# TensorE's unrolled program becomes a loop of seven turns over five heads, and the batch moves into partition halves

## The chip, the core and the metric

One core of a Trainium2 chip runs the kernel in one launch. The metric is device time in microseconds (us). Everything is fp32.

## The reference, cut to what matters

One decoding step for a batch of 2. The row x of 512 values is normalised. The attention has 32 heads of 128 values and looks at the last 2048 positions of a cache of 8192. A bilinear gated unit runs beside it, and both are added to x.

```python
q = (x @ wq).reshape(B, Sq, Hq, Dh)                  # B, Sq, D = 2, 1, 512; Hq, Dh = 32, 128
k, v = k_cache[:, :, Sk - W:, :], v_cache[:, :, Sk - W:, :]     # W = 2048
p = softmax(einsum("bhqd,bhkd->bhqk", q, k) * Dh ** -0.5)
o = einsum("bhqk,bhkd->bhqd", p, v)
attention = o.reshape(B, Sq, Hq * Dh) @ wo
glu = ((x @ w_gate) * (x @ w_up)) @ w_down           # F = 1376
xn = layernorm(x);  out = x + attention(xn) + glu(xn)
```

One head has 2 MB of keys and 2 MB of values for both batch elements together. 159.5 MB are read in all, and each value is used once.

## The kernel before, in words

**Data.** The host lays all inputs out as one stream in the order of use. `blocks()` (line 57) lists its blocks, `pump()` (line 297) loads them with one DMA each, issued by SP, into three slots of SBUF of 7.9 MB (`step`). The next load of a slot is issued when everything in it has been used (`done`, line 318). `KS` (line 40) says how many heads of keys each load has, one to three; values (`vp`) fill the rest, a few heads behind the keys. A small block `first` with x and a part of wq goes ahead of them.

**A head.** Each partition has 16 positions of each of the two batch elements. VectorE multiplies the keys by q, which TensorE has laid out over all partitions in PSUM (`products`, line 432), and adds up each position's 128 products (`sums`, line 440). `maxima` (line 445) takes the largest score of each partition and GpSimd the largest over all partitions; `weights` (line 453) has ScalarE form the exponentials p, and GpSimd their sum. `reciprocals` (line 468) follows one head later.

**Values.** TensorE multiplies p with the values, eight matmuls of 512 columns to a head (`weigh`, line 484), in four column groups of one bank. ScalarE copies the bank to SBUF (`copy_out`, line 494), TensorE adds the four groups up and turns them (`transpose`, line 501), ScalarE scales by the reciprocals (into `oT`), and TensorE multiplies by the head's rows of wo into `acc` (`project_o`, line 520). One or two heads share a pass (`groups`).

**q.** For four heads at a time, one head's share of wq at a time (`project_q`, line 415), straight into one of two PSUM banks from which VectorE reads.

**Order.** All engines' programs are written out. The order in which `products`, `sums`, `weigh` and so on are called is the order on each engine's queue; `Flow` (line 109) finds the data dependences and puts semaphore waits on the instructions. Ahead of the last heads the order is written by hand, from the line `h = H - 2` on, with `keep_busy` (line 481), matmuls whose results nobody reads. There, head 31's values are multiplied in two column halves into two banks, and the rest of w_down (`down`, line 605) follows.

Of the kernel before, what the change touches and what calls it, by code (L numbers as in the profile page):

```python
# [8 lines left out]
ALU = mybir.AluOpType  # L9
# [8 lines left out]
J = W // P  # L18
# [6 lines left out]
LAG = 3  # L25
# [5 lines left out]
HG = 4  # L31
GC = HG * DH
JG = J // 4
CK, CQ, CO = B * J * DH, NC * GC, D
CP = CQ // NC
UNIT = CK + max(CP, CO)
STEP = 31 * FB
NP = 6
NV = CK // FB
KS = [3, 1, 2, 1, 2, 2, 1, 2, 2, 2, 1, 2, 2, 2, 1, 2, 2, 1]  # L40
WD = [(0, 2), (2, 4), (4, 7), (7, NFC - 1), (NFC - 1, NFC)]
NS = 3
BUFS = 3
BASE = 30 * 1024
FX = FR // NS

# [10 lines left out]
def blocks():  # L57

    def wd(n):
        return [("wd", i, D) for i in range(*WD[n])]

    def k(h):
        return [("k", h, CK)] + ([("wq", h, CP)] if h + HG < H else [])  # L70

    def v(h):
        return [("v", h, CK), ("wo", h, CO)]

    def gu(half):
        n = NC * (FH[half][1] - FH[half][0])
        return [("wg", half, n), ("wu", half, n)]

    ones = [("pick", 0, 8 * B), ("rows", 0, NFB * B)]
    first = [("x", 0, B * NC)] + ones + [("w", 0, NC * DH)]  # L80
    ahead = [[("w", 1, CQ - NC * DH)], gu(0) + gu(1), [("wr", 0, NS * P)] + wd(0)]
    pieces = [(h, n) for h in range(H - 1 - LAG) for n in range(NV + 1)]
    loads, h = [], 0
    for i, n in enumerate(KS):
        fields = (ahead[i] if i < len(ahead) else []) + sum((k(h + j) for j in range(n)), [])
        h += n
        room = (STEP - sum(w for _, _, w in fields)) // FB if i > 1 else 0
        taken, pieces = pieces[:room], pieces[room:]
        for g in sorted({g for g, _ in taken}):
            assert g < h - n  # L90
            ns = [m for t, m in taken if t == g]
            parts = [m for m in ns if m < NV]
            if parts:
                p0, p1 = parts[0], parts[-1] + 1
                fields.append(("vp", (g, p0, p1), FB * (p1 - p0)))
            if ns[-1] == NV:
                fields.append(("wo", g, CO))
        assert not pieces or pieces[0][0] >= h - NP
        loads.append(fields)
    assert not pieces and h == H - 1  # L100
    loads += [k(H - 1) + v(H - 1 - LAG) + wd(1)]
    out = [(("f", 0), first)] + [(("s", i), fields) for i, fields in enumerate(loads)]
    late, last = ("s", len(loads)), ("s", len(loads) + 1)
    out += [(late, v(H - 3)), (late, v(H - 2)), (last, [("v", H - 1, CK)])]
    out += [(last, [("wo", H - 1, CO)] + wd(2))]
    return out + [(last, wd(n)) for n in range(3, len(WD))]


class Flow:
# [7 lines left out]
    def __init__(self, nc):  # L117
        self.nc = nc
        self.units = {
            "pe": nc.tensor, "dve": nc.vector, "act": nc.scalar, "pl": nc.gpsimd, "sp": nc.sync,  # L120
        }
        self.ops, self.seen, self.free = [], {}, {}
        self.low = -(-nc.sbuf_base // 32) * 32
# [38 lines left out]
    def add(self, unit, make, writes, reads):  # L162
        n = len(self.ops)
        deps = set()
        for aps, write in ((reads, False), (writes, True)):
            for ap in aps:
                if not isinstance(ap.tensor, (bass.SBTensorHandle, bass.PSumTensorHandle)):
                    continue
                name, p0, p1, f0, f1 = self.box(ap)
                kept = []  # L170
                for old in self.seen.get(name, []):
                    m, w, a0, a1, b0, b1 = old
                    if m != n and (write or w) and a0 < p1 and p0 < a1 and b0 < f1 and f0 < b1:
                        deps.add((m, w))
                        if write and p0 <= a0 and a1 <= p1 and f0 <= b0 and b1 <= f1:
                            continue
                    kept.append(old)
                self.seen[name] = kept + [(n, write, p0, p1, f0, f1)]
        self.ops.append((unit, make, deps))
# [3 lines left out]

    def emit(self):
        nc, ops = self.nc, self.ops
        place, count = [], {}
        for n, (unit, make, deps) in enumerate(ops):
            key = ("dma", n) if make[0] == "dma_start" else unit
            count[key] = count.get(key, 0) + 1
            place.append((key, count[key]))  # L190
        knows = [None] * len(ops)
        known = {unit: {} for unit in self.units}
        waits = []
        for n, (unit, make, deps) in enumerate(ops):
            have = known[unit]
            need = {}
            for m, wrote in deps:
                key, at = place[m]
                if key == unit and (unit == "pe" or unit in ("dve", "act") and not wrote):
                    continue  # L200
# [7 lines left out]
            ]  # L208
            for m in keep:
# [11 lines left out]
        told = {m for keep in waits for m in keep} | {len(ops) - 1}  # L221
        sems, value, at = {}, {}, {}
        order = sorted({place[m][0] for m in told}, key=lambda key: (key in ("dve", place[-1][0]), str(key)))
        if order[-1] != place[-1][0]:
            order.append(order.pop(-2))
        for key in order:
            sems[key] = nc.alloc_semaphore("done_" + (key if isinstance(key, str) else f"load{key[1]}"))
# [7 lines left out]
        for n, (unit, (method, args, kwargs), _) in enumerate(ops):  # L235
            eng = self.units[unit]
            keep = sorted(
                waits[n], key=lambda m: (isinstance(place[m][0], tuple) and m >= landed, m)
            )
            landed = max([landed] + [m for m in keep if isinstance(place[m][0], tuple)])  # L240
# [5 lines left out]
            if n in value:  # L246
                key = place[n][0]
                made.then_inc(sems[key], 16 if isinstance(key, tuple) else 1)
            if n == len(ops) - 2:
# [5 lines left out]
        nc.sync.wait_ge(end, 16).then_inc(end, -16)  # L255

# [15 lines left out]
def sliding_attention_plus_glu_kernel(  # L272
# [13 lines left out]
    ]  # L286


    todo, at = [], 0
    for key, fields in blocks():  # L290
        todo.append((key, fields, at))
        at += P * pitch(fields)
    tiles, used, left, got = {}, {}, {}, {}
    for key, fields, _ in todo:
        left[key] = left.get(key, 0) + len(fields)

    def pump():
        while todo:
            key, fields, at = todo[0]
            if key not in tiles:  # L300
                if key[0] == "f":
                    n = sum(w for _, _, w in fields)
                    tiles[key] = flow.tile([P, n], "first")
                elif not slots:
                    return
                else:
                    tiles[key] = slots.pop(0)
                used[key] = 0
            todo.pop(0)
            c0 = used[key]  # L310
            for kind, i, w in fields:
                got[kind, i] = (tiles[key][:, used[key] : used[key] + w], key)
                used[key] += w
            c1 = used[key]
            src = stream[at : at + P * pitch(fields)].rearrange("(p i) -> p i", p=P)
            sp.dma_start(tiles[key][:, c0:c1], src[:, : c1 - c0])

    def done(kind, i):
        _, key = got.pop((kind, i))
        left[key] -= 1  # L320
# [501 lines left out]
```

## Time and profile before

| What | Value |
|---|---|
| Time, median of 3 runs | 376.09 us (375.97 to 376.46) |
| Span of the profiled execution, first to last instruction | 374.6 us |
| TensorE busy | 248.4 us (66%), 1094 matmuls |
| VectorE busy | 295.1 us (79%) |
| ScalarE busy | 58.1 us (16%) |
| HBM read | 159.47 MB, 426 GB/s over the span |
| Mean granted TensorE clock | 0.813 |

The span is 1.5 us shorter than the median time; this much lies around it. The profile names the tiles without buffer numbers: `step` is any of the three slots, `q` the queries, `s` the scores, `m` and `mm` the maxima, `p` the exponentials, `o_ps` the bank for p times the values, `o_sb` its copy, `tr` the bank for transposes, `oT` the scaled outputs of a head, `acc` the sum in PSUM. An fp32 matmul of the program stands as two matmul records and two weight loads. PE is TensorE, PEld its weight loads, DVE VectorE, ACT ScalarE, POOL GpSimd, SP SyncE.

### The profile page before, as it was taken

Reading aid. Unit: us, or ns where it says so; the run is one execution under the profiler, and the core shown is the slowest. Engines: PE = TensorE matmul, PEld = TensorE weight load, DVE = VectorE, ACT = ScalarE, POOL = GpSimd, SP = SyncE. Lnnn points to the kernel's source line nnn. Section 1 sums busy time; section 2 is a strip of 40 time slices with the busy share of each in tenths; the row PEclk is TensorE's granted clock in tenths of the full one; section 3 lists DMA queues with packets and bytes.
Section 4 is the critical chain, followed back from the end, with each engine's and each line's share of the span. In section 5 each row is a group of like instructions: output and inputs, shape, how many; then the busy total and the mean of one; then the engine's idle time right before and its main releaser. Section 6 shows DMA issues by size and latency. Waiting matters only on the chain.

```text
span 374.6 us, 2741 instructions
## 1 busy us (share of the span) xinstructions
PE 248.4 (66%) x1094; PEld 86.8 (23%) x1094; DVE 295.1 (79%) x147; ACT 58.1 (16%) x259; POOL 25.3 (7%) x78
## 2 busy tenths in 40 slices
PE   3167675896578157855658585781488647476997
PEld 3033124231132013211212121320122112111344
DVE  3069998994599994599999945999999459999760
ACT  1002012111022012110202020300121201111232
POOL 1000000100001000000000000010001000000010
PEclk9759695898689758896969886998689868666999
DMA  8999999999999999999999999999999999999996
GB/s 345 420 465 454 450 432 435 434 434 424 427 427 434 434 434 434 436 434 441 434 435 429 434 434 434 434 429 434 434 435 434 429 434 434 428 426 416 414 432 250
DMA packets 3950, 159.70 MB, mean 426 GB/s; under 512 B 466, under 2 KB 610, under 8 KB 994
## 3 DMA queue, kind: packets, MB, share of 16 engines
q1 hardware_dynamic: 3938, 159.54, 98.6%
q8 instruction: 8, 0.13, 0.1%
q14 instruction: 4, 0.03, 0.0%
HBM read 159.47 MB, written 0.07 MB: 426 GB/s over the span
## 4 chain that ended last, share of the span: by engine, by line
DMA 64%; DVE 26%; PE 7%; ACT 1%; issue 0%; SPq 0%
DMA step<-in_stream_dram 64%; DVE s L243 13%; DVE step L243 13%; PE q L243 3%; PE acc L243 2%; PE o_ps L243 2%; PE tr L243 1%; ACT o_sb L243 0%; DVE m L243 0%; ACT oT L243 0%; DVE rec L243 0%; SPq L243 0%; DVE o_out L243 0%
## 5 line engine op out<-in xcount | busy, mean ns | idle before, releaser
L243 DVE TENSOR_TENSOR step<-step,q 128x4096 f32<-128x4096 f32 x31 | 136.8, 4411 | 47.0 <-DMA step<-in_stream_dram 47.0
L243 DVE TENSOR_REDUCE s<-step 128x32 f32<-128x4096 f32 x32 | 141.4, 4419 | 1.1
L243 PE MATMUL q<-step,xnb 128*128 128x512 f32 (+1 forms) x128 | 79.0, 759 | 80.5 <-DMA step<-in_stream_dram 80.5
L243 PE MATMUL o_ps<-step,p 128*16 128x512 f32 (+1 forms) x512 | 98.5, 730 | 11.2 <-DMA step<-in_stream_dram 11.2
L243 PEld LDWEIGHTS q<-step,xnb 128*128 128x128 f32 x128 | 28.0, 238 | 123.5 <-DMA step<-in_stream_dram 92.9
L243 PE MATMUL acc<-step,oT 128*9 128x512 f32 (+1 forms) x88 | 39.1, 604 | 8.7 <-ACT oT L243 8.7
L243 PE MATMUL tr<-first,o_sb 128*128 128x2 f32 (+2 forms) x198 | 29.1, 266 | 17.9 <-ACT o_sb L243 12.0
L243 PEld LDWEIGHTS tr<-first,o_sb 128*128 128x128 f32 x198 | 26.8, 205 | 40.6 <-ACT o_sb L243 31.3
L243 PEld LDWEIGHTS o_ps<-step,p 128*16 128x16 f32 x512 | 17.6, 107 | 78.6 <-issue 64.9
L243 ACT COPY o_sb<-o_ps 128x512 f32<-128x512 f32 (+1 forms) x24 | 13.8, 576 | 121.4 <-PE o_ps L243 121.4
L243 POOL PARTITION_ALL_REDUCE mm<-m x32 | 11.3, 355 | 268.6 <-DVE m L243 258.7
L243 ACT ACTIVATE nm<-mm 128x2 f32<-128x2 f32 x32 | 6.5, 203 | 148.0 <-POOL mm L243 148.0
L243 ACT ACTIVATE p<-s,nm 128x16 f32<-128x16 f32 x64 | 19.2, 300 | 1.0
L243 POOL PARTITION_ALL_REDUCE sum<-rs x32 | 12.7, 398 | 69.1 <-ACT p L243 69.1
L243 ACT ACTIVATE oT<-tr,rec 128x1 f32<-128x1 f32 x64 | 12.2, 260 | 27.0 <-PE tr L243 27.0
L243 DVE TENSOR_TENSOR step<-step,tr 128x4096 f32<-128x4096 f32 x1 | 4.4, 4422 | 14.8 <-DMA step<-in_stream_dram 14.8
L243 ACT ACTIVATION_READ_ACCUMULATOR p<-s,nm 128x1 f32 x64 | 11.9, 187 | 0.0
L243 PE MATMUL o_ps<-step,xn 128*2 128x512 f32 (+1 forms) x48 | 10.1, 548 | 0.0
L243 PEld LDWEIGHTS acc<-step,oT 128*9 128x9 f32 x88 | 4.6, 94 | 21.1 <-ACT oT L243 14.5
L243 DVE TENSOR_TENSOR o_out<-acc,x_nat 128x128 f32<-128x128 f32 x1 | 0.3, 292 | 8.4 <-PE acc L243 8.4
L243 DVE TENSOR_REDUCE m<-s 128x2 f32<-128x32 f32 x32 | 6.0, 186 | 1.1
L243 DVE RECIPROCAL rec<-sum 128x2 f32<-128x2 f32 x32 | 5.0, 155 | 1.9 <-POOL sum L243 1.9
(43 smaller groups left out, 41.5 us busy)
## 6 DMA issues: line engine op xcount, KB each, us to landing
step<-in_stream_dram SPq DMA_DIRECT2D x14, 7936.0 KB, 37.7
step<-in_stream_dram SPq DMA_DIRECT2D x2, 7680.0 KB, 32.0
step<-in_stream_dram SPq DMA_DIRECT2D x1, 7872.0 KB, 58.2
step<-in_stream_dram SPq DMA_DIRECT2D x1, 7808.0 KB, 38.8
step<-in_stream_dram SPq DMA_DIRECT2D x1, 4864.0 KB, 30.3
step<-in_stream_dram SPq DMA_DIRECT2D x2, 2304.0 KB, 19.6
step<-in_stream_dram SPq DMA_DIRECT2D x1, 2048.0 KB, 18.3
step<-in_stream_dram SPq DMA_DIRECT2D x1, 1024.0 KB, 19.8
```

The costliest lines, as they stand in the source:

```text
L243: made = getattr(eng, method)(*args, **kwargs)
```

## The change

**The loop.** TensorE's instructions between a prologue and an epilogue are written once, for one turn, and run by a register loop of seven turns. A turn has the parts q (queries of five heads), a, b and c (values of five heads); in the seventh only a runs, the others are under an `If`. Since each turn's instructions must be the same, every tile has a fixed place by the head's number modulo 5, every load a fixed slot and column, and TensorE waits for *tokens*: a semaphore of each waited-for engine that the other side counts up and TensorE counts down, in an instruction of its own ahead of the matmul. That a load has landed is told to TensorE by SP (`tell`: SP waits for the load, then counts up the token).

```diff
+            if part:
+                for key in sorted(points[part[0], part[2]]):
+                    eng.wait_ge(sems["token", key], 1).then_inc(sems["token", key], -1)
...
+            if method == "tell":
+                m = args[0]
+                eng.wait_ge(sems[place[m][0]], value[m]).then_inc(sems["token", unit], tokens[n])
+                return
...
+        with nc.tensor.Fori(0, max(turns.values())) as turn:
+            for section, ns in body.items():
+                short = turns[section] < max(turns.values())
+                with nc.tensor.If(turn < turns[section]) if short else contextlib.nullcontext():
+                    for n in ns:
+                        write(n)
```

**The loads.** Keys of heads 0 to 2 go ahead (`AHEAD`), then the gated unit's weights with the first wq; after that three loads of 7.9 MB to a turn. Turn t has the keys of heads 3+5t to 7+5t and the values of heads 5t to 5t+4. Its third load also has wq for the next turn. The last turn's end comes in smaller loads.

```diff
+    for t in range(T):
+        last = t == T - 1
+        out.append((0, 0, k(k0, k0 + 1) + vp(v0) + vp(v0 + 1, 0, VA)))
+        out.append((1, 0, k(k0 + 2, k0 + 3) + vp(v0 + 1, VA) + vp(v0 + 2) + vp(v0 + 3, 0, VB)))
+        b, c = vp(v0 + 3, VB), vp(v0 + 4)
+        if not last:
+            out.append((2, 0, [("wq", t + 1, CQ)] + k(k0 + 4) + b + c))
...
```

**The halves.** Partitions 0 to 63 have batch element 0, with 32 positions each, and 64 to 127 element 1. One q of 640 columns serves both; ScalarE copies it to SBUF (`q_sb`) and VectorE reads it from there. The maximum and the exponentials are formed for each half by itself.

```diff
-    dve.tensor_reduce(m, s, axis=AX.X, op=ALU.max)
+    for b, half in halves():
+        dve.tensor_reduce(m[half, b : b + 1], s_t[h][half, :], axis=AX.X, op=ALU.max)
...
+        act.copy(q_sb[t % 2], q_ps[:, :GC])
```

**The order of the calls.** `scores(h)` is `products`, `sums`, then a part of TensorE's work, then `maxima`, `weights` and `reciprocals(h - 1)`. The two passes of a turn are heads 5t, 5t+1 (in part b) and 5t+2 to 5t+4 (in part c). `keep_busy` is gone, and head 31's values use one bank.

```diff
+    for t in range(T):
+        part_q(t)
+        h = AHEAD + G * t
+        scores(h, lambda: part_a(t))
+        scores(h + 1)
+        scores(h + 2, lambda: part_b(t))
+        scores(h + 3)
+        if h + 4 < H:
+            scores(h + 4, lambda: part_c(t))
+        else:
+            reciprocals(h + 3)
+            part_c(t)
+    part_a(T)
+
+    down(HOLE)
...
+    weigh(H - 1, VA, NV)
+    o_sb = copy_out(0)
```

Three places show how the instructions stand now. The first is ScalarE's queue ahead of its last instructions, before the change: `p` are the exponentials, heads 30 and 31 in `p_57` and `p_58`.

```order
COPY o_sb_117<-o_ps 128x512 [waits done_pe]
ACTIVATE oT_63<-tr,rec_114 128x1 [waits done_dve,done_pe]
ACTIVATE oT_63<-tr,rec_114 128x1
ACTIVATE nm_92<-mm_86 128x2 [waits done_pl]
ACTIVATE p_57,rs_98<-s_74,nm_92 128x4x4 [waits done_act]
ACTIVATE p_57,rs_98<-s_74,nm_92 128x4x4
COPY o_sb_116<-o_ps 128x512 [waits done_pe]
ACTIVATE oT_64<-tr,rec_115 128x1 [waits done_pe]
ACTIVATE oT_64<-tr,rec_115 128x1
ACTIVATE nm_93<-mm_87 128x2 [waits done_pl]
ACTIVATE p_58,rs_99<-s_75,nm_93 128x4x4 [waits done_act]
ACTIVATE p_58,rs_99<-s_75,nm_93 128x4x4
```

The same place after the change (heads 30 and 31 again in `p_57` and `p_58`, then the copy of the last full pass, heads 27 to 29, its six scalings, and the copy of the pass of heads 30 and 31).

```order
ACTIVATE nm_94<-mm_88 128x2 [waits done_pl]
ACTIVATE p_57,rs_69<-s_82,nm_94 64x8x4 [waits done_act]
ACTIVATE p_57,rs_69<-s_82,nm_94 64x8x4
ACTIVATE nm_95<-mm_89 128x2 [waits done_pl]
ACTIVATE p_58,rs_70<-s_83,nm_95 64x8x4 [waits done_act]
ACTIVATE p_58,rs_70<-s_83,nm_95 64x8x4
COPY o_sb_107<-o_ps 128x512 [waits done_pe]
ACTIVATE oT<-tr,rec 128x1 [waits done_pe]
ACTIVATE oT<-tr,rec 128x1 x5
COPY o_sb_106<-o_ps 128x512 [waits done_pe]
```

Before, passes of earlier heads were copied and scaled ahead of and between the exponentials of the last heads; now the pass of heads 27 to 29 stands behind head 31's exponentials.

The second place is the end of a turn on TensorE: part c of the body, the branch back, and what follows the loop. (`done_tokensp` and `done_tokenact` are the tokens of SP and ScalarE.)

```order
MATMUL o_ps<-step_51,p_61 24x512 x7
MATMUL tr<-first,o_sb_107 128x6 [waits done_tokenact]
MATMUL tr<-first,o_sb_107 128x6 x3
MATMUL acc<-step_50,oT 9x512 [waits done_tokenact]
MATMUL acc<-step_51,oT 9x512 [waits done_tokenact] x2
UNCONDITIONAL_BRANCH
REGISTER_ALU
COMPARE_AND_BRANCH
MATMUL acc<-step_51,hT 9x512
MATMUL o_ps<-step_50,p_58 16x512 [waits done_dma835]
MATMUL o_ps<-step_50,p_58 16x512 x2
```

At the same place before, between the two last full passes and the rest, there was no branch, and values of later heads stood between the passes.

```order
MATMUL o_ps<-step_51,p_60 16x512 x8
MATMUL tr<-first,o_sb_117 128x2 x4
MATMUL q<-xnb,mean_w 128x256
MATMUL tr<-first,o_sb_116 128x4 x4
MATMUL acc<-step_51,oT_64 9x512
MATMUL acc<-step_51,oT_65 9x512
MATMUL acc<-step_51,oT_66 9x512
MATMUL q<-xnb,mean_w 128x256
MATMUL o_ps<-step_49,p_61 16x512 x8
MATMUL acc<-step_49,hT 9x512 x2
MATMUL tr<-first,o_sb_117 128x2 x4
```

The third is ahead of the loop and at its top, on TensorE now: the gated unit (`o_ps<-step_51,xn` and what follows) stands ahead of the first wq.

```order
MATMUL o_ps<-step_51,xn 2x352 x8
MATMUL tr<-first,o_sb_107 128x6 [waits done_dve]
MATMUL tr<-first,o_sb_107 128x6 [waits done_act] x6
MATMUL acc<-step_51,hT 9x512 x2
MATMUL acc<-step_51,hT 9x384
MATMUL acc<-step_51,hX 9x128 x2
MATMUL acc<-step_51,hX 9x128 [waits done_act]
UNCONDITIONAL_BRANCH
COMPARE_AND_BRANCH
MATMUL q<-step_51,xnb 128x512 [waits done_tokensp]
MATMUL q<-step_51,xnb 128x128
```

Before, at that place:

```order
MATMUL q<-step_49,xnb 128x384 x8
MATMUL q<-step_49,xnb 128x512 x6
MATMUL q<-step_50,xnb 128x512 x2
MATMUL o_ps<-step_50,xn 2x512 x16
MATMUL o_ps<-step_50,xn 2x352 x8
MATMUL tr<-first,o_sb_117 128x6 x7
MATMUL q<-step_51,xnb 128x512 x2
```

The queries of heads 1 to 3 and most of the next four heads' stood ahead of the gated unit, and the others followed a head at a time.

More of the change, by code (lines that the diff above doesn't have):

```diff
@@ L82, in blocks @@
[L82 to L106, printed above, removed]
+    def k(*heads):
+        return [("k", h, CK) for h in heads]
+    def vp(h, p0=0, p1=NV):
+        return [("vp", (h, p0, p1), FB * (p1 - p0))] + ([("wo", h, CO)] if p1 == NV else [])
@@ L675, in sliding_attention_plus_glu_kernel, with scores @@
[L675 to L683 removed]
+    def scores(h, then=None):
+        products(h)
+        sums(h)
+        if then:
+            then()
+        maxima(h)
+        weights(h)
+        if h >= 1:
+            reciprocals(h - 1)
+    project_first()
+    for h in range(AHEAD):
+        scores(h)
+    for half in range(2):
+        project_gu(half)
```

612 lines of the change are left out of this document (312 added, 300 removed).

## The prediction

> **What bounds the kernel now.** I read the page first, then the busy time by windows, then the chain that ended last, then the timeline of the end.
>
> ```profile
> span 374.6 us, 2741 instructions
> DMA  8999999999999999999999999999999999999996
> q1 hardware_dynamic: 3938, 159.54, 98.6%
> q8 instruction: 8, 0.13, 0.1%
> DMA 64%; DVE 26%; PE 7%; ACT 1%; issue 0%; SPq 0%
> step<-in_stream_dram SPq DMA_DIRECT2D x14, 7936.0 KB, 37.7
> ...
> 60.00:340.00 280.00, 184.13 (x715) 57.98 (x714) 234.72 (x102) 42.95 (x203) 19.21 (x51) 0.80 1.00 434
> ```
>
> The DMA engines are busy in every slice. From 60 to 340 us (last row: PE, PEld, DVE, ACT, POOL busy, clock, DMA share, GB/s) their share is 1.00 at 434 GB/s, so 159.5 MB need about 368 us. A load of 7.9 MB lands 37.7 us after its issue but takes 18.7 us at this rate: a whole load lies queued ahead of it, and the stream doesn't wait for the engines. The 26% of VectorE in the chain are only the steps from a load to the issue of the next.
>
> So the time is the stream plus what is left when the last byte has landed.
>
> ```profile
> 372.26 0.12 PEld L243 LDWEIGHTS acc<-step,hT 128*9 128x9 f32 x8 [0.22 <-DMA step<-in_stream_dram]
> 372.74 0.29 DVE L243 TENSOR_TENSOR o_out<-acc,x_nat 128x128 f32<-128x128 f32 x1 [8.38 <-PE acc L243]
> 373.05 0.35 SPq L243 DMA_DIRECT2D out_dram<-o_out  x1
> ```
>
> The last load lands at 372.2, the result is formed 0.5 us later (372.74), and the span ends 1.9 us after that. The heads are done by then. Nothing is to be gained in the stream but its last tenths; what the change can do is lose, where work is left behind the last byte.
>
> **The change, part by part.** *Stream:* the same bytes in the same order, give or take 0.01 MB. The smaller TensorE program saves at most the 0.13 MB of the instruction queue, 0.3 us at 434 GB/s. I count E, the last landing, as 372.2 again.
>
> *A head on VectorE.*
>
> ```profile
> 40.07 4.40 DVE L243 TENSOR_TENSOR step<-step,q 128x4096 f32<-128x4096 f32 x1
> 44.51 4.42 DVE L243 TENSOR_REDUCE s<-step 128x32 f32<-128x4096 f32 x1
> 48.96 0.19 DVE L243 TENSOR_REDUCE m<-s 128x2 f32<-128x32 f32 x1
> 49.06 0.15 DVE L243 RECIPROCAL rec<-sum 128x2 f32<-128x2 f32 x1
> 49.13 4.40 DVE L243 TENSOR_TENSOR step<-step,q 128x4096 f32<-128x4096 f32 x1
> ```
>
> One head takes 49.13 - 40.07 = 9.06 us, 8.9 of it to the end of the sums. The products keep their shape (q from SBUF is not in the trace; the same element count, so I take the same 4.40). The maximum becomes two instructions: at least 0.1 us more a head, the offset of the next row here, at most 0.35 if none overlap. I take 0.2: 9.26 us. Here the row shows the reciprocal starting at 49.06, while the maximum (to 49.15) still runs. The Trainium skill (VectorE: DVE Perf Modes, section on two Vector instructions with no wait between them) says that an instruction whose input starts in another quadrant of partitions is held until every earlier one has finished; by that rule the overlap goes for the second half and for what follows it, the 0.35 end, and the sum below would be 0.5 us higher.
>
> A turn thus needs 5 x 9.26 = 46.3 us of VectorE, and its three loads (23.6 MB) 54.4 us of stream.
>
> *The end.* Behind the load with the keys of heads 28 and 29, `blocks()` puts 36,864 columns of 512 bytes: the keys of 30 and 31 with values, then values of 28 to 31, wo and w_down. That is 18.9 MB, 43.5 us: this load lands at 372.2 - 43.5 = 328.7. VectorE then has four heads: 3 x 9.26 + 8.9 = 36.7, so head 31's sums are done at 365.4 at the earliest, 4 us later than before.
>
> ```profile
> 361.44 0.19 DVE L243 TENSOR_REDUCE m<-s 128x2 f32<-128x32 f32 x1
> 361.72 0.35 POOL L243 PARTITION_ALL_REDUCE mm<-m  x1 [2.62 <-DVE rec L243]
> 362.16 0.20 ACT L243 ACTIVATE nm<-mm 128x2 f32<-128x2 f32 x1
> 362.89 0.19 ACT L243 ACTIVATION_READ_ACCUMULATOR p<-s,nm 128x1 f32 x1
> ```
>
> From the maximum to the end of the exponentials it is 363.08 - 361.44 = 1.64; with the second maximum 1.75: 367.15.
>
> Now comes what decides. On ScalarE the copy of the pass of heads 27 to 29 stands behind head 31's exponentials. Their values have landed (12,800 columns or 15 us ahead of E) and TensorE has multiplied them, but the bank can't be copied. TensorE waits there with all that follows in its order: the transposes, three `project_o`, the whole of part a of the seventh turn (13 matmuls on head 30 and 31), then the rest. All this lay beside the stream before; now it starts at 367.15 and runs one thing after the other.
>
> ```profile
> 102.87 0.59 ACT o_sb L243
> 103.47 0.04 issue
> 103.51 1.07 PE tr L243 x8
> ...
> 104.60 0.42 ACT oT L243 x2
> ...
> 135.15 3.78 PE L243 MATMUL q<-step,xnb 128*128 128x512 f32 x4 [12.11 <-DMA step<-in_stream_dram]
> ...
> 154.38 1.98 PE L243 MATMUL q<-step,xnb 128*128 128x512 f32 x4
> ...
> 354.48 1.88 PE L243 MATMUL acc<-step,hT 128*9 128x512 f32 x4
> ...
> 363.05 1.91 PE L243 MATMUL o_ps<-step,p 128*16 128x512 f32 x16
> ...
> 370.83 0.84 PE L243 MATMUL acc<-step,hT 128*9 128x128 f32 x24
> ```
>
> Copy to transpose 103.51 - 102.87 = 0.64; transpose to scaling 104.60 - 103.51 = 1.09; two scalings and the start of the next matmul about 0.47. A product with wo has two records of 1.88/4 = 0.47, 0.9 us, so three are 2.7. That is at full clock: after 12 us of waiting the same four records of q take 3.78 instead of 1.98, and here TensorE has waited for 6 us with no `keep_busy`. Between 2.7 and 5.2 I take 4.0. Part a: 13 matmuls at 1.91/8 = 0.24, 3.1. `down(HOLE)` 0.9. The last three on head 31's values 0.7, copy 0.64, transpose 1.1 (the scaling lies under the next twelve matmuls). Then 36 matmuls of 128 columns at 0.84/12 = 0.07: 2.5. Sum 0.64 + 1.09 + 0.47 + 4.0 + 3.1 + 0.9 + 0.7 + 0.64 + 1.1 + 2.5 = 15.1, and the result is formed at 367.15 + 15.1 + 0.1 = 382.4 instead of 372.74: 9.7 us later. Without any waiting clock it would be 1.3 less.
>
> *Tokens.* Waits are instructions of their own on TensorE now, some eight in this stretch; the trace has none in a chain. Between nothing and 0.15 us each (VectorE's small row): 0.8. On SP a `tell` that waits for a landing has the next loads' issues behind it. A slot's reload waits for the wo of its last head: slot 1 for head 5t+2's `project_o` in part c, about 10 us after the third load of the turn has landed, with 18.1 us of the next load as cover. Nothing, while ScalarE isn't late there; if that cover is gone, each us over is a us of stream.
>
> *The start.* The gated unit's weights come in one load with the first wq, and TensorE has to do all of it before q.
>
> ```profile
> 44.13 10.05 PE L243 MATMUL o_ps<-step,xn 128*2 128x512 f32 x48
> ...
> 58.64 0.60 PE L243 MATMUL tr<-first,o_sb 128*128 128x6 f32 x2 [4.45 <-DVE o_sb L243]
> ...
> 64.35 0.15 ACT L243 COPY hX<-tr 32x2 f32<-32x2 f32 x1 [0.69 <-PE tr L243]
> ```
>
> That load lands near 37 us (14.8 MB). 10.05 for the matmuls and 2.5 more at a cold start: 49.5. Copy and product 1.3, the seven steps 64.50 - 58.64 = 5.9, `down` 2.5, q (four pairs at 0.99 + 0.3) 5.2, its copy to SBUF (640 columns) 0.75: VectorE starts head 3 near 65, when its keys (22.6 MB) have lain there since 55. Ten us behind, with the reloads of slots 0 and 1 just in time: 0.5 us of stream, between none and 2.
>
> *The turn.* In a late turn ScalarE again copies part c's pass behind the fourth head's exponentials, and q follows: 36.7 + 1.75 + 0.64 + 1.09 + 0.47 + 2.7 to 5.2 + 5.2 + 0.75 = 49.3 to 51.8 us from q to q. The stream takes 54.4, so VectorE catches up 2.6 to 5.1 a turn, 13 to 25 in five: by head 28 it is level, as assumed above.
>
> Sum: 9.7 + 0.8 + 0.5 = 11.0 us. 376.09 + 11.0 = **387.1 us**. (The profiled span of 374.6 would become 385.6; the 1.5 around it stay.)
>
> **The rivals.** *The turn becomes the bound.* If a turn takes longer than 54.4, the lag of 10 us never goes and each turn adds. What could: the branch back. The body has 61 matmuls of four instructions and the waits and branches, some 265; before the change, instructions came over a DMA queue of their own, in 8 packets of 16 KB (0.13 MB). The Trainium skill (Runtime: NRT & Kernel Launch, section on instruction fetch) says that a branch to a place outside the two pages held makes the sequencer fetch it before it goes on, so that a body of over 256 instructions would pay at every turn; no row of before has a branch. Its price from rows: between nothing and a small load's landing behind the row of a big one (the 271 KB of `first` took 2.8 us, a row of 62 KB on one of 16 engines 2.3), 5 us, of which some 2 hide under the last `project_o`.
>
> ```profile
> first<-in_stream_dram SPq DMA_DIRECT2D x1, 271.0 KB, 2.8
> ```
>
> With 51.8 + 3 = 54.8 a turn, head 28 starts at 65 + 5 x 54.8 = 339 instead of 328.7, and all ends 10 us later: 397. It decides from 3 us a turn. For it: the load on the queue is full. Against: the last token is taken before the last `project_o` is through.
>
> *The end is shorter.* TensorE stays at full clock (-1.3), waits cost nothing (-0.8), no start bubble (-0.5), and up to 1.5 less from overlap that rows of single steps don't show: 383.
>
> *Faster.* The end doesn't count. This needs head 31's exponentials 10 us earlier than I have them, that is VectorE at 6.8 us a head instead of 9.26, with q now in SBUF instead of PSUM. Then the result follows the last landing by 0.5 as now, less the 0.3 of the instruction queue: 375.8. It decides from the four heads: the rows of the sums (4.42), which never read PSUM, speak against it.
>
> **How the numbers follow.** The forecast 387.1 has 0.6 (384.5 to 391), the long turn 0.22 (391 to 405), the short end 0.13 (381.5 to 384.5), no difference 0.02, faster 0.03. A measurement of this kernel can tell about 0.2%, 0.75 us. Range: 382 to 401. Faster by over 0.2%: 0.03, within: 0.02, slower: 0.95.
>
> **What would show it.** After the change, the last load lands near 372 but the result is formed some 10 us later; the chain ends in ScalarE's copy of `o_sb`, `tr`, `acc`, and before them VectorE's four heads back to a landing near 329 (forecast) or to the copy of q (long turn). In the window from 60 to 340 the DMA share stays at 1.00 (forecast) or falls (long turn). VectorE's head has 9.2 to 9.4 us. The first `q_sb` copy ends near 65. Wrong I am if head 31's exponentials end before 360, if part c's copy doesn't wait for them, or if VectorE waits for q in the last turns without a long branch.

## The result, and the profile after the change

The changed kernel takes 407.72 us (median of 4 runs, 405.88 to 409.46) against 376.05 (375.97 to 376.46): 1.084 times as long, 95% interval 1.080 to 1.087. The forecast was slower, 387.1 in a range of 382 to 401. The direction is right; the time lies outside the range, and 31.7 us were lost where 11.0 were forecast. Times here are medians of the fast runs: one run of the tenth and one of the eleventh experiment, 1.6% and 1.7% above the fastest of its kernel, are left out as slow.

The page of the changed kernel, with the lines that answer to those of before:

```profile
span 405.6 us, 2602 instructions
DMA  9999999985999999999998999999999999998392
q1 hardware_dynamic: 4226, 159.54, 93.2%
q8 instruction: 2, 0.03, 0.0%
L317 POOL PARTITION_ALL_REDUCE mm<-m x32 | 110.0, 3436 | 226.1 <-DVE m L317 226.1
```

The stream's share has gone from 98.6% to 93.2%; it dips at a quarter of the span (5) and near its end (3). The instruction queue has shrunk. The row of GpSimd is the one that the prediction had not looked for: 32 maxima over the partitions take 3436 ns each in the mean. Before, a tenth of that:

```profile
L243 POOL PARTITION_ALL_REDUCE mm<-m x32 | 11.3, 355 | 268.6 <-DVE m L243 258.7
```

The window of the middle stretch (PE, PEld, DVE, ACT, POOL busy, clock, DMA share, GB/s) and the result, from the timeline of the end:

```profile
60.00:340.00 280.00, 133.07 (x611) 48.87 (x611) 231.70 (x123) 42.14 (x183) 103.86 (x48) 0.71 0.96 407
```

```profile
403.69 0.29 DVE L317 TENSOR_TENSOR o_out<-acc,x_nat 128x128 f32<-128x128 f32 x1 [1.95 <-PE acc L317]
```

The share falls from 1.00 to 0.96, the prediction's own sign for a long turn. The row of the result starts at 403.69; the forecast's 382.4 counts to the start of the same row (372.74 before). The last load lands near 398 and not near 372: the DMA share is 0.94 from 396 to 398 us and 0.08 in the two us after.

VectorE's first product of a turn, from its timeline; the row in brackets says what it waited for:

```profile
66.10 4.43 DVE L317 TENSOR_TENSOR step<-step,q_sb 128x4096 f32<-128x4096 f32 x1 [15.39 <-ACT q_sb L317]
123.39 4.43 DVE L317 TENSOR_TENSOR step<-step,first 128x4096 f32<-128x4096 f32 x1 [10.28 <-ACT first L317]
...
350.99 4.43 DVE L317 TENSOR_TENSOR step<-step,first 128x4096 f32<-128x4096 f32 x1 [10.44 <-ACT first L317]
```

(The second buffer of `q_sb` lies in the tile `first`.) Head 3 starts at 66.1, near the 65 of the forecast. Five turns later head 28 starts at 351.0 instead of 328.7: (350.99 - 66.10) / 5 = 57.0 us a turn, where the forecast had 49.3 to 51.8, and from the second turn on VectorE waits 9 to 10.4 us for the copy of q. The lag of the start never goes, and each turn adds 57.0 - 54.4 = 2.6 us to it.

What happens in such a turn, from its fourth head on (timeline of all engines, 160 to 181 us; POOL is GpSimd):

```profile
160.44 0.37 DVE L317 TENSOR_REDUCE m<-s 64x1 f32<-64x32 f32 x2
...
160.91 4.64 POOL L317 PARTITION_ALL_REDUCE mm<-m  x1 [3.15 <-DVE m L317]
160.93 4.41 DVE L317 TENSOR_TENSOR step<-step,first 128x4096 f32<-128x4096 f32 x1
...
165.59 0.20 ACT L317 ACTIVATE nm<-mm 128x2 f32<-128x2 f32 x1 [8.31 <-POOL mm L317]
...
166.68 0.59 ACT L317 COPY o_sb<-o_ps 128x512 f32<-128x512 f32 x1
...
167.41 1.85 PE L317 MATMUL tr<-first,o_sb 128*128 128x6 f32 x8 [7.38 <-PEq L309]
...
169.85 5.28 PE L317 MATMUL acc<-step,oT 128*9 128x512 f32 x6 [0.59 <-PEq L309]
...
170.30 0.36 POOL L317 PARTITION_ALL_REDUCE mm<-m  x1 [3.15 <-DVE m L317]
...
175.06 4.70 PE L317 MATMUL q<-step,xnb 128*128 128x512 f32 x16
179.79 0.69 ACT L317 COPY q_sb<-q 128x640 f32<-128x640 f32 x1 [8.04 <-PE q L317]
```

The fourth head's maximum over the partitions begins with the fifth head's products and ends with them: 160.91 + 4.64 = 165.55, and the products end at 165.34. So it is with 23 of the 32 maxima, 4.64 each; beside the other nine no products with q from SBUF run, and they take 0.36. The fifth head's maximum, at 170.30, when VectorE has nothing to multiply, takes 0.36. Behind the first stand in a row the exponentials, ScalarE's copy of the pass, the transposes, three products with wo, the next q and its copy, and then VectorE. From the maximum (160.44) to the end of the exponentials (166.65) it is 6.2 us, where the forecast had 1.75. The next q begins as the last product with wo ends (175.1): no time is seen at the branch.

### The profile page after: what moved, and what is told of

Read it like the earlier page. It is cut to its first block, busy times and chain, and to the rows that moved or that the text cites. A ratio compares the mean times of both kernels' runs of the same rounds, so it can differ in the third digit from the quotient of the medians.

```text
span 405.6 us, 2602 instructions
## 1 busy us (share of the span) xinstructions
PE 197.9 (49%) x940; PEld 72.2 (18%) x940; DVE 302.5 (75%) x179; ACT 59.5 (15%) x250; POOL 124.4 (31%) x84
## 3 DMA queue, kind: packets, MB, share of 16 engines
q1 hardware_dynamic: 4226, 159.54, 93.2%
## 5 line engine op out<-in xcount | busy, mean ns | idle before, releaser
L317 POOL PARTITION_ALL_REDUCE mm<-m x32 | 110.0, 3436 | 226.1 <-DVE m L317 226.1
L317 PE MATMUL o_ps<-step,p 128*24 128x512 f32 (+1 forms) x512 | 81.9, 668 | 64.4 <-PEq L309 64.4
L317 DVE TENSOR_TENSOR step<-step,q_sb 128x4096 f32<-128x4096 f32 x15 | 66.1, 4408 | 35.6 <-ACT q_sb L317 35.6
L317 DVE TENSOR_TENSOR step<-step,first 128x4096 f32<-128x4096 f32 x14 | 61.7, 4409 | 29.7 <-ACT first L317 29.7
L317 PE MATMUL tr<-first,o_sb 128*128 128x6 f32 (+1 forms) x118 | 25.9, 338 | 101.3 <-PEq L309 98.9
L317 PEld LDWEIGHTS o_ps<-step,p 128*24 128x24 f32 (+1 forms) x512 | 18.0, 104 | 112.4 <-issue 112.2
L317 PE MATMUL q<-step,xnb 128*128 128x512 f32 (+1 forms) x96 | 28.0, 445 | 0.0
L317 ACT ACTIVATE p<-s,nm 64x32 f32<-64x32 f32 x64 | 20.4, 319 | 1.4
L317 PEld LDWEIGHTS q<-step,xnb 128*128 128x128 f32 x96 | 15.2, 195 | 19.2 <-issue 19.2
L317 ACT ACTIVATE oT<-tr,rec 128x1 f32<-128x1 f32 x60 | 10.4, 266 | 24.4 <-PE tr L317 24.4
L317 ACT ACTIVATION_READ_ACCUMULATOR p<-s,nm 64x1 f32 x64 | 11.8, 185 | 0.0
```

What stands on the lines that cost most here:

```text
L317: made = getattr(eng, method)(*args, **kwargs)
```

## The experiments

Theory A: reading both operands of the products from SBUF holds up GpSimd while the products run; the late maximum makes the turn longer than the stream, and the rest is the forecast's own. Theory A' is that each held maximum costs a part. Theory B: the maximum is slow because of the -3.0e38 (`LOW`) with which the change fills half of `m`. Theory C: the loop, its tokens and its branch make the turn long. The experiments have the numbers of the order in which they ran, and stand here by what they are about.

### 1: q in PSUM, where VectorE read it before

The copy of q goes to two free banks of PSUM; nothing else is changed.

```diff
-    q_sb = [flow.tile([P, GC], "q_sb"), first[:, sum(w for _, _, w in blocks()[0][2]) - NC * FIRST :][:, :GC]]
+    q_sb = [flow.bank([P, 4 * FB // 2], "q_copy")[:, :GC]] * 2
```

> The changed kernel, with ScalarE's copy of the five heads' queries written to two free PSUM banks instead of SBUF; everything else, the loop and the copy itself included, stays. Theory A (VectorE's products with both operands in SBUF hold up GpSimd's maximum over the partitions): every mm takes 0.36 us again instead of 4.64, the exponentials of a turn's fourth head end about 1.9 us after its maximum instead of 6.2, a turn falls from 57.0 to about 52.7 us, below the 54.4 of its three loads, and the time to 386 us (383 to 389), which is the forecast's own mechanism. Theory B (the slow maximum comes from the data, the -3.0e38 in the other halves of m): mm stays at 4.64 and the time at 407. Theory C (the loop itself, its tokens and branch, makes the turn long): mm may fall, but the time stays over 400.

Measured: 392.74 us (390.12 to 394.19), 1.042 of before (1.037 to 1.047). All maxima, from the view of the tile `mm` (duration ns least, median, most):

```profile
L317 POOL PARTITION_ALL_REDUCE mm<-m x32: 354/354/355, 29.1 to 370.8; - x32
```

The first products of the turns, from VectorE's timeline:

```profile
66.66 4.42 DVE L317 TENSOR_TENSOR step<-step,q_copy 128x4096 f32<-128x4096 f32 x1 [15.56 <-ACT q_copy L317]
...
118.57 4.42 DVE L317 TENSOR_TENSOR step<-step,q_copy 128x4096 f32<-128x4096 f32 x1 [4.92 <-ACT q_copy L317]
...
333.31 4.42 DVE L317 TENSOR_TENSOR step<-step,q_copy 128x4096 f32<-128x4096 f32 x1 [7.40 <-DMA step<-in_stream_dram]
```

The late turn now takes 118.57 - 66.66 = 51.9 us, just above the forecast's 49.3 to 51.8, and by the last turn VectorE waits for the stream and no longer for q. 15.0 of the 31.7 us go with the long maxima. (In the two traces head 28 starts 17.7 us earlier, 333.3 instead of 351.0, and what follows head 31's exponentials takes 5.0 us longer, of which more below.) B and C fall as causes of these 15. But the time was expected at 386, and 6.7 us more were left, which the later experiments place.

### 2: other data

```diff
-LOW = -3.0e38
+LOW = -1.0e4
```

> The changed kernel with the halves of m that no maximum is written to filled with -1e4 instead of -3.0e38. Theory A (two operands in SBUF): nothing changes, mm has the same two durations, 0.36 and 4.64, and the time is 407.7 (405 to 410). Theory B (the data make the maximum slow): mm is 0.36 throughout and the time 386.

Measured: 406.88 us (405.59 to 407.98), 1.082 of before (1.079 to 1.085). The tile `mm` again:

```profile
L317 POOL PARTITION_ALL_REDUCE mm<-m x32: 354/4638/4642, 29.2 to 388.6; - x32
```

As in the changed kernel, whose row says 356/4640/4643. Theory B is out.

### 3: the same in the kernel before

ScalarE copies the q of the first two heads of each four to SBUF, into the used part of `first`; the other two heads' q stays in PSUM.

```diff
+    q_sb = got["w", 0][0].rearrange("p (b n) -> p b n", b=B)
...
+        if c == NC - 1:
+            act.copy(q_sb, q_ps[g][:, :, : 2 * DH])
...
+        if g and hh < 2:
+            qb = q_sb[:, :, hh * DH : (hh + 1) * DH]
```

> The kernel before, in which ScalarE copies the queries of the first two heads of each four to SBUF and VectorE reads these from there, the other two still from PSUM. Theory A: the mm of a head whose follower's products read q from SBUF (heads 3, 4, 7, 8, ...) takes 4.6 us, the others stay at 0.355; the products stay at 4.40, and the time stays within 1 us of 376.1, since the stream covers it here. Theory B: all mm stay at 0.355 in this kernel, which has no -3.0e38 and no halves.

Measured: 376.01 us (375.82 to 376.36), 1.000 of before (0.999 to 1.001). Two heads from the timeline, one of each kind:

```profile
106.79 4.41 DVE L243 TENSOR_TENSOR step<-step,first 128x4096 f32<-128x4096 f32 x1
106.89 4.52 POOL L243 PARTITION_ALL_REDUCE mm<-m  x1 [16.94 <-DVE m L243]
...
125.49 4.40 DVE L243 TENSOR_TENSOR step<-step,q 128x4096 f32<-128x4096 f32 x1
125.59 0.35 POOL L243 PARTITION_ALL_REDUCE mm<-m  x1 [4.51 <-DVE m L243]
```

In one kernel, without loop, halves or fill, the maximum is held beside products with q from SBUF and not beside those with q from PSUM, while the products take the same time (4.41, 4.40). And it costs nothing here: with the stream a whole load ahead, nobody waits for these exponentials. Not every head that was named was held: where VectorE waited for a load between the maximum and the products, the maximum had 0.35, and the sum that follows it was held instead (3.71 us at 117.37).

### 4: the loop undone

TensorE's program is written out, with ordinary waits.

```diff
-        self.part = (section, t)
-        self.count.setdefault(self.part, 0)
         yield
-        self.part = None
...
-        with nc.tensor.Fori(0, max(turns.values())) as turn:
...
+            write(n)
```

> The changed kernel with TensorE's program written out: no register loop, no branch, no tokens and no telling by SP, with ordinary waits on the instructions; tiles, loads and the order of the calls stay. Theory A: the turn stays within 0.5 us of 57.0 and the time at 406 to 408, with the bytes of the instruction queue back at 0.1 MB or more. Theory C (the loop costs some us a turn): the turn falls to 54.4 or below, and the time to 400 or less.

Measured: 407.15 us (406.45 to 407.64), 1.083 of before (1.081 to 1.085). VectorE's timeline at two turns:

```profile
123.09 4.43 DVE L314 TENSOR_TENSOR step<-step,first 128x4096 f32<-128x4096 f32 x1 [10.15 <-ACT first L314]
180.23 4.43 DVE L314 TENSOR_TENSOR step<-step,q_sb 128x4096 f32<-128x4096 f32 x1 [10.13 <-ACT q_sb L314]
```

57.1 us a turn, as with the loop (180.59 - 123.39 = 57.2). Theory C is out, and with it the branch of the rival *the turn becomes the bound*: loop and tokens together cost 0.6 us by the medians, less than the runs' own spread.

### 5: one of five

Only the fifth head's products read q from PSUM.

```diff
+        if h >= AHEAD and n == G - 1:
+            q = q_ps[:, n * DH : (n + 1) * DH]
```

> The changed kernel, in which only the products of a turn's fifth head read q from TensorE's bank in PSUM; the other four still read it from SBUF. Theory A says that just one of the slow maxima is on the path: the fourth head's, which runs beside the fifth head's products and stands ahead of ScalarE's copy of the turn's last pass. So mm of the fourth head is 0.36 us again, those of the first three stay at 4.64, and the time is that of the copy in PSUM, 393 (390 to 396). Theory A' (each slow maximum costs some of the 15 us): a fifth to a quarter of it comes back, 403 to 405.

Measured: 393.59 us (392.25 to 394.77), 1.046 of before (1.042 to 1.049). GpSimd's maxima of the third and fourth head of a turn, from the timeline:

```profile
145.61 4.64 POOL L317 PARTITION_ALL_REDUCE mm<-m  x1 [3.15 <-DVE m L317]
...
154.99 0.36 POOL L317 PARTITION_ALL_REDUCE mm<-m  x1 [3.15 <-DVE m L317]
```

14.1 of the 15.0 us come back, though only five of the 23 long maxima have become short, one in a turn. The other three of a turn are still held, and what they cost, 0.9 us by the medians, is less than the runs' spread: only the fourth head's stands ahead of the copy for which TensorE waits.

### 12: a wait put in

q stays in SBUF, and VectorE waits for the fourth head's maximum before it starts the fifth head's products.

```diff
         maxima(h)
+        if h >= AHEAD and (h - AHEAD) % G == G - 2:
+            dve.tensor_copy(flow.ring([P, B], "seen", 2), mm_t[h])
```

> The changed kernel as it is, q in SBUF, with one small VectorE instruction more in a turn: after the fourth head's maximum it copies mm, two values, to a tile that nobody reads, so that the fifth head's products start only when GpSimd is done. Theory A (which of the two starts first decides who is held): mm of the fourth head takes 0.36 us and the others 4.64; VectorE loses 0.6 to 0.8 us a turn, which a late turn pays and an early one doesn't; the time is 393 to 396, so that a wait put in brings back some 13 of the 15 us. Rival (reading q from SBUF slows GpSimd in another way than by the products that run beside it): mm stays at 4.64 there and the time at 407 or above.

Measured: 394.75 us (391.42 to 394.97), 1.047 of before (1.042 to 1.052). The same place in the timeline:

```profile
158.26 0.36 POOL L317 PARTITION_ALL_REDUCE mm<-m  x1 [3.15 <-DVE m L317]
...
158.65 0.17 DVE L317 COPY seen<-mm 128x2 f32<-128x2 f32 x1 [0.48 <-POOL mm L317]
...
158.80 4.41 DVE L317 TENSOR_TENSOR step<-step,first 128x4096 f32<-128x4096 f32 x1
...
159.81 3.66 POOL L317 PARTITION_ALL_REDUCE sum<-rs  x1 [1.19 <-ACT p L317]
```

The maximum is over at 158.62, before the products begin. Half a us of waiting on VectorE brings back 13 us. The hold has moved to the sum (3.66), which only the scaling needs, later. So it counts which of GpSimd's instructions is held, and what waits for it.

### 7: q ahead of the gated unit

With the copy in PSUM, TensorE forms the first five heads' q before the gated unit.

```diff
     for h in range(AHEAD):
         scores(h)
+    project_q(0)
...
-        with flow.loop("q", t):
-            project_q(t)
+        if t:
+            with flow.loop("q", t - 1):
+                project_q(t)
```

> As the first experiment, and TensorE forms the first five heads' q ahead of the gated unit instead of behind it (the other turns' q stand at the end of the turn before). Theory A: VectorE starts head 3 when its keys have landed, near 56 instead of 66.7; the stream's gap near 90 us goes, heads 28 and 29 land near 329 instead of 333.3, and the time falls by 4 to 5 us, to 388 (386.5 to 390). Rival: the stream's loss comes from elsewhere (the order of the reloads), then the landing stays at 333 and the time at 392 to 393.

Measured: 388.74 us (387.42 to 389.72), 1.035 of before (1.032 to 1.038). VectorE's timeline and the window after it:

```profile
55.62 4.42 DVE L317 TENSOR_TENSOR step<-step,q_copy 128x4096 f32<-128x4096 f32 x1
...
329.32 4.42 DVE L317 TENSOR_TENSOR step<-step,q_copy 128x4096 f32<-128x4096 f32 x1 [7.51 <-ACT q_copy L317]
```

```profile
60.00:120.00 60.00, 38.05 (x160) 11.36 (x158) 51.01 (x28) 8.81 (x39) 3.77 (x10) 0.79 0.99 427
```

The same window of the kernel with the copy in PSUM alone:

```profile
60.00:120.00 60.00, 34.72 (x166) 13.29 (x168) 47.85 (x26) 9.39 (x39) 3.76 (x10) 0.77 0.96 407
```

The late start costs 4.0 us, where the forecast had 0.5 and at most 2; head 28 starts at 329.3 instead of 333.3. In this window it is 2 to 3 us of stream: 1.8 by the shares of 0.96 and 0.99, 2.8 by 407 and 427 GB/s. Where the rest is lost is not shown.

### 6: the order at the end

With the copy in PSUM, the last part c is called ahead of head 31's exponentials.

```diff
-        scores(h + 3)
         if h + 4 < H:
+            scores(h + 3)
             scores(h + 4, lambda: part_c(t))
         else:
+            scores(h + 3, lambda: part_c(t))
             reciprocals(h + 3)
-            part_c(t)
```

> As the first experiment (copy of q in PSUM), and in the last turn part c is called between head 31's sums and its maximum, so that ScalarE copies and scales the pass of heads 27 to 29 ahead of head 31's exponentials. Theory A with the end as forecast: three transposes and products with wo and the values of head 30 leave the path behind the exponentials, which end at about 372.3 of the span as before; from there 13 matmuls (3 to 5 us), the last part of w_down that waits for them, 1.0, and the same 6.9: the result 6 to 8 us earlier, 386 (384 to 388) against 392.7. Rival: TensorE's values of heads 28 and 29 are themselves late (their load), then 390 to 393.

Measured: 385.27 us (381.38 to 386.06), 1.021 of before (1.015 to 1.027). From the timeline:

```profile
365.92 0.59 ACT L317 COPY o_sb<-o_ps 128x512 f32<-128x512 f32 x1 [3.85 <-PE o_ps L317]
366.65 1.03 PE L317 MATMUL tr<-first,o_sb 128*128 128x6 f32 x8 [0.78 <-PEq L309]
...
370.39 0.20 ACT L317 ACTIVATE nm<-mm 128x2 f32<-128x2 f32 x1 [1.65 <-POOL mm L317]
```

The pass of heads 27 to 29 is copied and transposed before head 31's maximum is there, and 7.5 us go. What the forecast said of this place, that the copy stands behind those exponentials and everything on TensorE behind the copy, is borne out.

### 8 and 11: TensorE kept busy

With the copy in PSUM, unread matmuls ahead of the second pass's transposes: twelve, then five.

```diff
+    def keep_busy():
+        pe.matmul(q_ps[:, :FB], mean_w, spare_in, start=True, stop=True)
...
+        o_sb = copy_out(group)
+        for _ in range(12 * group):
+            keep_busy()
+        d = transpose(group, o_sb)
```

> As the first experiment, with twelve matmuls of 512 columns that nobody reads ahead of the transposes of each turn's second pass, where TensorE waits for ScalarE's copy. If the end is longer than forecast because TensorE's clock is low after its wait (transposes 1.85 us instead of 1.05, one row of wo or values 0.43 instead of 0.24): 2 to 4.5 us less, 389.5 (388 to 391). Rival: the clock granted doesn't follow the work just ahead, or the twelve stand in the way: 392 to 396.

> As the eighth experiment with five unread matmuls instead of twelve. The twelve took 10.6 us, 0.88 each, since TensorE had the low clock through all of them; five take 4.4, and TensorE waits 6 us there. If the clock after a wait is what makes the end 4 us longer than forecast: 389.5 (388 to 391). If five are too few to raise it, or they stand in the way in other turns: 392 to 396.

Measured: twelve 406.36 us (405.45 to 408.69), 1.083 of before (1.079 to 1.086); five 390.56 (389.11 to 393.91), 1.037 (1.034 to 1.039), which can't be told from the 392.74 (390.12 to 394.19) without any. The twelve lie outside both ranges of their expectation; the runs with five spread over both. The twelve in the last turn, from TensorE's timeline:

```profile
378.94 10.57 PE L317 MATMUL q<-xnb,mean_w 128*128 128x512 f32 x24
```

One unread matmul has two records of 0.44, so twelve take 10.6 us. The reason given in the second expectation, the low clock, is wrong: the clock granted in this stretch was 1.00. They stood in the way in every turn: in the trace VectorE waits 5.6 to 11.6 us for q from the second turn on, and 13.6 us are lost again. What they were meant to show is seen by comparing kernels whose last 136 matmuls are the same and differ in the clock. The windows from the end of head 31's exponentials to the result (clock, DMA share, GB/s at the end of each row): the changed kernel, then q ahead of the gated unit, then the copy in PSUM alone.

```profile
390.00:404.00 14.00, 11.52 (x136) 5.48 (x136) 1.30 (x4) 2.19 (x8) 0.40 (x1) 1.00 0.57 238
```

```profile
368.30:384.50 16.20, 13.72 (x136) 6.46 (x136) 1.30 (x4) 2.19 (x8) 0.40 (x1) 0.82 0.22 91
```

```profile
372.30:391.30 19.00, 16.52 (x136) 7.40 (x136) 1.30 (x4) 2.19 (x8) 0.40 (x1) 0.68 0.20 82
```

The same work takes 14.0, 16.2 and 19.0 us. TensorE stands idle for 2.5 us in each of the three (14.00 - 11.52 in the first), though in the first the stream still runs beside it; the whole difference is in its busy time. In the trace with five the clock fell all the same (below).

### 9 and 10: together

The copy in PSUM, q ahead of the gated unit and the order at the end, with the three edits shown above.

> The copy of q in PSUM, the last part c ahead of head 31's exponentials, and the first q ahead of the gated unit: the first, sixth and seventh experiments together. If the three causes are apart, their gains add: 392.7 - 4.0 - 7.5 = 381.3 (380 to 383). If the load with head 29's values (it landed near 360 in the seventh) now holds the end, less: 383 to 385.

Measured: 381.06 us (380.02 to 381.62), 1.013 of before (1.011 to 1.016). The three causes are apart, and their gains add. Then the last turn's part c and the values of heads 30 and 31 were taken out of the loop as well:

```diff
+    def part_end():
...
+        o_sb = copy_out(1)
+        weigh(H - 2, 0, NV)
+        scale_out(1, transpose(1, o_sb))
+        for n in SPLIT[1]:
+            project_o(G * t + n)
+        down(HOLE)
...
+    weigh(H - 1, 0, VA)
     weigh(H - 1, VA, NV)
     o_sb = copy_out(0)
     accumulate(carry, acc_sb)
+    chunks = [c for group in TAIL for c in group]
+    for c in chunks[:-1]:
+        down(c)
     d = transpose(0, o_sb)
```

> As the ninth, with the last turn's part c and the values of heads 30 and 31 taken out of the loop and written out by hand: head 30's values are multiplied while ScalarE copies the pass of heads 27 to 29, the HOLE chunk follows the products with wo, and only head 31's eight matmuls, the copy, the transposes, two rows of wo and the last chunk of w_down stand behind head 31's exponentials, near 368. From there 1.9 + 0.7 + 1.1 + 0.2 + 0.6 + 0.6 = 5.1: the result near 373.5 and the time 377 (376 to 379), close to before, whose 376.05 the stream sets. Rival: TensorE's work ahead of head 31's values isn't done by 368, then 379 to 381.

Measured: 379.5 us (378.22 to 382.3), 1.011 of before (1.005 to 1.018): not told apart from the one before it, and not the 377 expected but the rival's 379 to 381. From its timeline:

```profile
367.04 2.74 PE L317 MATMUL acc<-step,oT 128*9 128x512 f32 x6 [0.50 <-ACT oT L317]
...
369.62 0.62 PE L317 MATMUL o_ps<-step,p 128*16 128x512 f32 x3
...
374.05 1.06 PE L317 MATMUL tr<-first,o_sb 128*128 128x4 f32 x8
```

Head 31's values wait for the products with wo until 369.6, and the chunks of w_down put ahead of the transposes hold these up to 374.05. None of the versions beats the kernel before.

## Why the prediction was wrong, point by point

The loss of 31.7 us, by the differences of the medians: the held maximum 407.7 - 392.7 = 15.0, the late start 392.7 - 388.7 = 4.0, the order at the end 388.7 - 381.1 = 7.7, and the rest 381.1 - 376.1 = 5.0, in which TensorE still has work behind head 31's exponentials (from 368.4 to 377.3 in that kernel's trace). The runs of one of these changed kernels spread over 1.6 to 4.1 us, so each part is good to a us or two.

- **"q from SBUF ... the same element count, so I take the same 4.40"** is the step that failed. The products did take 4.41. But the step priced the instruction for its own engine alone and didn't ask whom it holds up: beside it GpSimd's maximum went from 0.35 to 4.64. No product of before reads both operands from SBUF, so no row there has this price. The Trainium skill (SBUF — State Buffer, sections on the two separate sides and on who interferes with whom) says that a VectorE instruction with two inputs in SBUF contends with a GpSimd instruction that reads SBUF, and that the one which starts second is blocked for the whole of the first. The trace agrees on the contention: 4.64 and 4.52 beside products of 4.41, 0.35 beside products that read q from PSUM. On the order it agrees in the third experiment (products at 106.79, maximum at 106.89) and not in the changed kernel, where GpSimd's record starts 0.02 us ahead of the products and it is still GpSimd that is held.
- **"The turn ... 36.7 + 1.75 + ..."**: through this the 1.75 became 6.2, and the turn 57.0 instead of 49.3 to 51.8. With q in PSUM it was 51.9, so the other terms held in their sum, at the upper end (not each by itself: the transposes took 1.84 and not 1.09). Of the 5 us between the two turns some 4.3 are this step; the rest is mostly the three products with wo, 5.28 in the turn shown above and 4.01 with q in PSUM. The prediction's own sign of being wrong, that "VectorE waits for q in the last turns without a long branch", is what came.
- **The rival "the turn becomes the bound"** had the right consequence and the wrong cause. By its own rule, with 57.0 a turn, head 28 starts at 65 + 5 x 57.0 = 350, 21.3 later than 328.7, and 387.1 + 21.3 = 408.4; measured 407.7. That these lie so close is in part luck: the 408.4 hold 0.8 for tokens and 0.5 for the start, and an end of 15.2 us that took 13.7 (389.97 to 403.69). The branch, its only mechanism, cost nothing that could be measured. The Trainium skill's rule on a branch out of the two pages held (Runtime: NRT & Kernel Launch, section on instruction fetch) would, as the prediction read it, have made this body pay in every turn; here q follows `acc` without a gap, and the instruction queue moved 2 packets instead of 8. Whether the branch left the pages held, no run shows.
- **"A head on VectorE 9.26"**: 9.38 from one product to the next (151.55 and 160.93 in the timeline of that turn), 0.32 more than before and near the 0.35 end. The rule quoted there (the Trainium skill, VectorE: DVE Perf Modes, section on two Vector instructions with no wait between them) is borne out. The two maxima from 160.44 end at 160.81, and the reciprocal starts at 160.85, where before it started under the maximum. Over the last four heads it is 0.5 us.
- **"The end ... 15.1"**: the mechanism was right and is borne out by the order at the end. The size hangs on the clock: the forecast allowed for a low one only in the products with wo, and the same work took 14.0 at 1.00, 16.2 at 0.82 and 19.0 at 0.68. 9.7 + 0.8 were forecast for the whole; by the medians above it is 7.7 + 5.0 = 12.7.
- **"The start ... 0.5 us of stream, between none and 2"**: VectorE starts at 66.1 (65 forecast), but it costs 4.0. The cover was taken to be just in time, with no row to show it.
- **"Tokens 0.8"**: the written-out program takes 407.15, 0.6 less, which the runs' spread hides.

## What to carry to other kernels

Moving an operand from PSUM to SBUF can leave an instruction's own time as it is and change what runs beside it: look in the trace for short instructions of GpSimd whose record ends with a long one of VectorE. What a held instruction costs is set by what stands behind it in the queues, nothing where a load lies ahead, 15 us over this kernel's turns where a chain across four engines closes on it; and then one small wait that puts the short instruction first brought back 13 of them. A turn of a software loop has to be summed as a closed ring, from q to q, with each term checked for what the change puts beside it.

## What the runs showed of the hardware that was not expected

GpSimd's record starts ahead of the products (160.91 and 160.93) and is held nevertheless; it ends 0.2 us after them. In these traces GpSimd's instruction is held wherever its record overlaps products with both operands in SBUF, from 0.03 us ahead of their start to 1.0 us behind it (the sum of the twelfth experiment, 159.81 against 158.80), and never beside products with q from PSUM (0.40 us at most). In the twelfth experiment the maximum was over (158.62) before the products began (158.80), so that a lead of half a us was enough; what a shorter lead would do, no run shows. Nor does any show VectorE held: its products took 4.40 to 4.43 us in all of them.

TensorE's clock at the end of the kernel with the copy in PSUM (TensorE idle from 367.0, busy from 373.0; the clock is the third number from the end):

```profile
368.00:370.00 2.00, 0.00 (x0) 0.00 (x0) 2.00 (x1) 0.00 (x0) 0.00 (x0) 1.00 0.97 410
370.00:372.00 2.00, 0.00 (x0) 0.00 (x0) 0.84 (x4) 0.75 (x4) 0.35 (x1) 0.71 1.04 437
372.00:374.00 2.00, 0.97 (x5) 1.00 (x5) 0.17 (x1) 0.86 (x3) 0.40 (x1) 0.50 0.98 415
378.00:380.00 2.00, 2.00 (x10) 0.42 (x9) 0.00 (x0) 0.00 (x0) 0.00 (x0) 0.50 0.01 2
382.00:384.00 2.00, 2.00 (x18) 0.51 (x11) 0.00 (x0) 0.00 (x0) 0.00 (x0) 1.00 0.04 8
```

And with five unread matmuls, which end at 371.0:

```profile
366.00:371.00 5.00, 5.00 (x16) 1.82 (x10) 4.88 (x4) 0.00 (x0) 0.14 (x1) 1.00 0.99 417
371.00:373.00 2.00, 0.04 (x1) 0.00 (x0) 0.16 (x1) 1.61 (x6) 0.61 (x2) 1.00 1.05 444
374.00:380.00 6.00, 5.41 (x16) 1.40 (x16) 0.00 (x0) 1.02 (x6) 0.00 (x0) 0.50 0.34 138
```

In the first the clock falls inside the idle stretch: a mean of 0.71 from 370 to 372, read as one step from 1.00 to 0.50, puts it near 370.8, 3.8 us after the last matmul. In the second an idle stretch of 2.0 us (371.0 to 373.1) was enough, and the clock fell when the work was there again: 0.84 from 372 to 374 puts it near 373.4. In both it then stays at half through 6 us of nearly steady work. What sets the moment, these runs don't settle.
